# Retention followed by a squared-ReLU FFN: the second FFN product of seven blocks done as seven quarter products

## The chip, the cores and the metric

One core of one Trainium2 chip. A time is the device time of one execution in microseconds; lower is better. Engines: TensorE (PE; its weight loads are shown as PEld), VectorE (DVE), ScalarE (ACT), GpSimd (POOL) and SyncE (SP), which issues all of this kernel's DMAs. Each engine works through its own queue in the order in which the program was written.

## The reference

Four batches, eight heads, 768 steps, head size 64. A recurrent state is decayed and updated at each step, the result is laid out as 3072 tokens of 512 numbers, and a feed-forward network follows:

```python
for t in range(S):
    state = gamma[None, :, None, None] * state + np.einsum('bhd,bhe->bhde', k[:, :, t], v[:, :, t])
    y[:, :, t] = scale * np.einsum('bhd,bhde->bhe', q[:, :, t], state)
...
x = np.ascontiguousarray(attn_out.transpose(0, 2, 1, 3)).reshape(B * S, H * D)
h = np.maximum(x @ w_in, 0.0)          # w_in 512 x 2048
return (h * h @ w_out).astype(np.float32)   # w_out 2048 x 512
```

q, k, v, the weights and the result are fp32.

## The kernel before, in words

**Tiling.** The tokens are cut into 24 chunks of 128, six to a batch. `BLOCKS` groups them for the FFN: one block of four chunks (tb = 0) and ten of two (tb = 1 to 10). A chunk's attention is done in the chunked form: scores times mask, times v, plus q times the state so far. The matmuls take bf16 operands and sum in fp32 in PSUM.

**The order.** It is written out by hand. `ffn_pieces(tb)` (L786) is a generator; each `yield` ends a *place*, and `before(n)` (L984) then emits whatever `put` has entered for place n, and after it the squares of `take_squares` (L734). Places are numbered through: a two-chunk block has 16, block 1 those from 33 on, block 3 from 65, block 4 from 81, block 9 from 161. In such a block the first eight pieces are the first product: eight matmuls of 128 x 256 columns into one PSUM buffer (`first_product`, L754), then a ReLU on ScalarE (`relu`, L765) and a square on VectorE. The other eight are the second product: two chunks x 16 matmuls of 512 columns (`second`, L812), with a copy out of PSUM on ScalarE and a store behind each chunk (`store`, L823). The last eight places of a block thus take four 512-column matmuls each.

**Buffers.** PSUM has one buffer each for `tp`, `st`, `y` and `c_ps` and four in turn for `psf`, which both products use. `stage` is four fp32 buffers in turn, for the weights and for k and v of the later chunks.

**Attention from chunk 8 on** (`attend2`, L928), by d, the place of the chunk's outputs (70, 78, 86 and so on for chunks 10, 11, 12): q is scaled at d - 19 and d - 18 (even chunks), k at d - 18 (`scale_k2`, L618, VectorE, two instructions of 64 partitions, into a block-diagonal `ks_bdp`), v is cast at d - 15 (`cast_v2`, L631, POOL: once in full and twice by halves into a block-diagonal `v_bd`), k is transposed by DMA at d - 13, the state is updated at d - 6 and d - 3 (`state2`, L678; its PSUM is copied out by halves, one on ScalarE, one on VectorE), the scores are taken at d - 5 and the outputs at d.

**Loads.** k and v of three or four chunks come in eight DMAs (`batch_loads`, L120), one at each of the places in the table `places` (L971): chunks 15 to 17 of v at places 82 to 89, chunks 21 to 23 of v at 128 to 137. All wait in SP's queue among the transposes, the q loads and the stores.

**The weights of the second product** arrive in four quarters (`load_w_out`, L154; w_out rows in 16 blocks of 128) and are cast to bf16 at places 13, 17, 21 and 26 (`cast_w_out`, L300). Chunks 4 to 7 are attended in an earlier form (`attend`, L916; `scale_kv` L345, `transpose_k` L374, `scores` L396), and their items stand at places 21 to 49.

Of the kernel before, what the change touches and what calls it, by code (L numbers as in the profile page):

```python
# [22 lines left out]


PACK_FROM = 8


@with_exitstack
def kernel(
# [30 lines left out]
    const = ctx.enter_context(tc.tile_pool(name="const", bufs=1))  # L60
# [10 lines left out]

    stage = ctx.enter_context(tc.tile_pool(name="stage", bufs=4))
    opool = ctx.enter_context(tc.tile_pool(name="opool", bufs=4))
    ps_tp = ctx.enter_context(tc.tile_pool(name="ps_tp", bufs=1, space=bass.MemoryType.PSUM))
# [65 lines left out]
    halves = [slice(0, 64), slice(64, 128)]  # L140
    w_in_v = moe_w_in.rearrange("(cb p) f -> p cb f", p=P)
    w_out_v = moe_w_out.rearrange("(fb p) n -> p fb n", p=P)
    staged = {}
# [8 lines left out]
        staged["in", g] = t  # L152

    def load_w_out(g):  # L154
        t = stage_tile(FPQ * DM).rearrange("s (f n) -> s f n", f=FPQ)
        nc.sync.dma_start(t[:], w_out_v[:, g * FPQ : (g + 1) * FPQ, :])
        staged["out", g] = t

    load_q(0)
    load_pair(0, "kn", k, raw_k)  # L160
# [14 lines left out]
    def exponents(pattern, step, name, logs, parts=(slice(0, P),)):  # L175
# [27 lines left out]
        out=ident[:],  # L203
# [11 lines left out]
        out=cmask[:],  # L215
# [10 lines left out]
    for rows in halves:  # L226
        nc.gpsimd.affine_select(
            out=maskp[rows],
# [8 lines left out]
    kf2 = const.tile([P, NCH, 2, NPAIR], FP32)  # L237
# [44 lines left out]

    w_in_bf = [const.tile([P, NCB, FQ], BF16, name=f"w_in_bf{g}") for g in range(NQ)]
    w_out_bf = [const.tile([P, FPQ, DM], BF16, name=f"w_out_bf{g}") for g in range(NQ)]

    def cast_w(kind, g, halves=(0, 1), on="VVSG"):

# [327 lines left out]
            nc.vector.tensor_copy(to, fr)  # L615


    def scale_k2(m):  # L618
        b, i = chunks[m]
        ks = ks_bd2s[m % 2]  # L620
        kn = raw_k.pop(m)
        for hh, rows in enumerate(halves):
            nc.vector.tensor_tensor(  # L623
                out=ks[rows, :, hh, :].rearrange("s (u p) d -> s u p d", u=2),
                in0=kn[rows],
                in1=kf2[rows, i, :, :, None].to_broadcast([64, 2, NPAIR, D]),
                op=ALU.mult,
            )
        at[m]["ks"] = ks

    def cast_v2(m):  # L631
        vn = raw_v.pop(m)
        v2 = v2pool.tile([P, 2 * NPAIR, D], BF16, name="v2")
        nc.gpsimd.tensor_copy(v2.rearrange("s (u p) d -> s u p d", u=2), vn)  # L634
        v_bd = v_bd2s[m % 2]
        for hh, rows in enumerate(halves):
            nc.gpsimd.tensor_copy(  # L637
                v_bd[rows, :, hh, :].rearrange("s (u p) d -> s u p d", u=2), vn[rows]
            )
        at[m].update(v2=v2, v_bd=v_bd)  # L640

    def transpose_k2(m):
# [35 lines left out]
    def state2(m, u):  # L678

        b, i = chunks[m]  # L680
        a = at[m]
        if i == NCH - 1 and u == 1:
            return
        if i == 0 and u == 0:
            c_ps[0] = ps_c.tile([P, NPAIR, D], FP32, name="c_ps")
        c = c_ps[0]
        for p in range(NPAIR):
            nc.tensor.matmul(  # L688
                c[:, p, :],
                lhsT=a["ks"][:, u * NPAIR + p],  # L690
                rhs=a["v2"][:, u * NPAIR + p, :],
                start=(i == 0 and u == 0 and p == 0),
                stop=True,
                skip_group_check=True,
            )
        s_bd = s_bds[(2 * m + u) % 3]
        nc.scalar.activation(s_bd[halves[0], :, 0, :], c[halves[0]], AF.Copy)  # L697
        nc.vector.tensor_copy(s_bd[halves[1], :, 1, :], c[halves[1]])  # L698

    def outputs2(m):  # L700
        b, i = chunks[m]
# [30 lines left out]
    squares = []  # L732

    def take_squares():  # L734
        while squares:
            hv = squares.pop(0)
            nc.vector.tensor_mul(hv, hv, hv)  # L737


    h2s = {}  # L740
# [8 lines left out]
    def h_of(tb, f0, f1=None):  # L749
        n = NFB // len(h2s[tb])  # L750
        j, f = divmod(f0, n)
        return h2s[tb][j][:, f : f + (1 if f1 is None else f1 - f0)]
# [9 lines left out]
                stop=(cb == NCB - 1),  # L762
            )

    def relu(hv, hp):  # L765
        nc.scalar.activation(hv, hp[:], AF.Relu)  # L766
        squares.append(hv)

    open_ps = {}

# [15 lines left out]
    def ffn_pieces(tb):  # L786
        nch = BLOCKS[tb]
        TB = nch * C
        if tb == 0:
            for f in range(FPQ, NFB):  # L790
                hp = ps_f.tile([P, TB], FP32, name="psf")
                first_product(tb, hp[:], f, slice(0, TB))
                relu(h_of(tb, f)[:, 0], hp)
                yield
        elif tb <= 2:

            for c in range(nch):
                for g in range(NQ):
                    first_unit(tb, g, c)
                    yield  # L800
        else:
            h_tiles(tb)
            per = 512 // TB
            for f0 in range(0, NFB, per):
                hp = ps_f.tile([P, per, TB], FP32, name="psf")
                for f in range(f0, f0 + per):
                    first_product(tb, hp[:, f - f0, :], f, slice(0, TB))
                relu(h_of(tb, f0, f0 + per), hp)
                yield


        def second(op, j, g, cols=slice(0, DM)):  # L812
            for fq in range(FPQ):
                f = g * FPQ + fq
                nc.tensor.matmul(  # L815
                    op[:],
                    lhsT=h_of(tb, f)[:, 0, j * C : (j + 1) * C],
                    rhs=w_out_bf[g][:, fq, cols],
                    start=(f == 0),
                    stop=(f == NFB - 1),  # L820
                )

        def store(op, j, cols=slice(0, DM)):  # L823
            osb = opool.tile([P, DM], FP32, name="osb")
            nc.scalar.activation(osb[:, cols], op[:], AF.Copy)  # L825
            r0 = (first[tb] + j) * C
            nc.sync.dma_start(out[r0 : r0 + C, cols], osb[:, cols])
# [82 lines left out]
    def put(place, what, *args):  # L910
        parts.setdefault(place, []).append((what, args))
# [16 lines left out]
    def attend2(m, d, before, q_at, qturn_at, k_at, turn_at, v_at):  # L928
        if m % 2 == 0:
            put(q_at, scale_q, m, 0)  # L930
            put(q_at + 1, scale_q, m, 1)
            put(qturn_at, dma_transpose_q, m)
        put(k_at, scale_k2, m)
        put(v_at, cast_v2, m)
# [91 lines left out]
```

## Time and profile before

| | us |
|---|---|
| three runs | 213.21, 213.47, 214.4 (median 213.47) |
| the profiled execution: span from the first to the last instruction | 213.3 |
| TensorE busy / weight loads busy | 205.2 / 141.4 |
| VectorE / ScalarE / POOL busy | 134.7 / 117.0 / 57.9 |
| mean granted TensorE clock | 0.998 |

A span is read with its stages in mind: the first 20 us load and start, from 30 us on the FFN runs with attention between its pieces, and the last block has no attention beside it. In a line of the timeline the first number is the start, the second the time taken by the whole group, the bracket the idle time of that engine before it and what ended it. A matmul's time is longer than its distance to the next, since matmuls are pipelined; SPq is the time that SP spends on issuing.

### The profile page before, as it was taken

The numbers are of one execution on the slowest core, as the hardware profiler recorded it, in microseconds if no ns is written. First come the engines' busy times: TensorE is split into PE (matmuls) and PEld (weight loads), VectorE is DVE, ScalarE is ACT, GpSimd is POOL, SyncE is SP. The second block draws the span as 40 slices with busy tenths as digits, with TensorE's granted clock in tenths as the row PEclk, the third lists the DMA queues.
The fourth block names the chain that finished last, engine by engine and source line by source line (L and its number), as shares of the span: only waits on it lengthen the run. The fifth ranks groups of instructions, "written<-read, shape, count | busy, mean of one in ns | idle before, by whom it ended". The sixth has DMA issues, their size and how long they took to land.

```text
span 213.3 us, 5243 instructions
## 1 busy us (share of the span) xinstructions
PE 205.2 (96%) x2117; PEld 141.4 (66%) x2117; DVE 134.7 (63%) x263; ACT 117.0 (55%) x220; POOL 57.9 (27%) x114
## 2 busy tenths in 40 slices
PE   5798999999999999999999999999999999999994
PEld 1467744457965984884875875874965965965853
DVE  4677787235798997396495596595694793640410
ACT  8345887158953763662663663652753754643631
POOL 5232458223102523142230343052130433000000
PEclk9999999999999999999999999999999999999999
DMA  5999999999999997969978998959988451701102
GB/s 163 292 318 383 383 384 252 285 242 293 247 160 175 259 167 140 254 111 231 189 124 152 271 166 205 242 105 190 239 150 211 103 98 49 101 0 52 49 0 98
DMA packets 92727, 40.18 MB, mean 188 GB/s; under 512 B 68512, under 2 KB 86176, under 8 KB 92704
## 3 DMA queue, kind: packets, MB, share of 16 engines
q1 hardware_dynamic: 92704, 39.86, 83.1%
q8 instruction: 16, 0.26, 0.5%
q14 instruction: 7, 0.06, 0.1%
HBM read 27.26 MB, written 6.29 MB: 157 GB/s over the span
## 4 chain that ended last, share of the span: by engine, by line
PE 78%; DVE 8%; SPq 5%; DMA 4%; ACT 3%; issue 1%; ACTq 0%; DVEq 0%
PE psf L815 34%; PE psf L757 33%; SPq L132 4%; DMA kn<-in_k_dram 3%; DVE ks_bdp L623 2%; DVE h L737 2%; DMA stage<-in_v_dram 2%; PE y L717 2%; PE y L710 2%; PE st L661 2%; PE c_ps L688 1%; PE y L316 1%; PE c_ps L565 1%; DVE pt L548 1%; PE psf L524 1%
## 5 line engine op out<-in xcount | busy, mean ns | idle before, releaser
L757 PE MATMUL psf<-xt,w_in_bf 128*128 128x256 bf16 (+2 forms) x880 | 90.6, 259 | 0.2 <-ACT xt L488 0.2
L815 PE MATMUL psf<-w_out_bf,h 128*128 128x512 bf16 (+2 forms) x400 | 89.6, 371 | 0.0
L757 PEld LDWEIGHTS <-w_in_bf 128*128 128x128 bf16 x880 | 71.1, 98 | 11.6 <-issue 0.3
L766 ACT ACTIVATE h<-psf 128x512 bf16<-128x512 f32 x96 | 57.1, 597 | 22.2 <-PE psf L757 19.4
L815 PEld LDWEIGHTS <-h 128*128 128x128 bf16 x400 | 36.0, 98 | 35.7 <-DVE h L737 1.0
L737 DVE TENSOR_TENSOR h<-h 128x512 bf16<-128x512 bf16 x96 | 45.1, 492 | 17.8 <-ACT h L766 17.2
L698 DVE CAST s_bd<-c_ps 64x256 bf16<-64x256 f32 x29 | 12.4, 427 | 31.1 <-ACT s_bd L697 30.8
L637 POOL CAST v_bd<-stage 64x512 bf16<-64x512 f32 x32 | 23.2, 726 | 28.1 <-PE y L717 27.1
L825 ACT ACTIVATE osb<-psf 128x512 f32<-128x512 f32 (+2 forms) x25 | 14.5, 580 | 28.8 <-PE psf L815 28.8
L634 POOL CAST v<-stage 128x512 bf16<-128x512 f32 x16 | 11.3, 705 | 61.7 <-DMA stage<-in_v_dram 28.8
L623 DVE TENSOR_TENSOR ks_bdp<-stage,kf 64x512 bf16<-64x512 f32 x32 | 24.9, 779 | 0.6
L724 ACT ACTIVATE xt<-y 128x512 bf16<-128x512 f32 x16 | 11.9, 741 | 13.5 <-PE y L717 13.5
L335 DVE TENSOR_TENSOR qs<-qn,qf 128x512 bf16<-128x512 f32 x22 | 15.4, 709 | 2.3 <-DMA qn<-in_q_dram 2.0
L697 ACT ACTIVATE s_bd<-c_ps 64x256 bf16<-64x256 f32 x29 | 10.6, 367 | 10.3 <-PE c_ps L688 8.1
L411 DVE TENSOR_TENSOR pt<-st,cmask 128x512 bf16<-128x512 f32 x8 | 5.5, 689 | 10.1 <-PE st L404 10.1
L668 DVE TENSOR_TENSOR pt<-st,cmask 128x512 bf16<-128x512 f32 x16 | 11.1, 691 | 0.5
L304 POOL CAST w_out_bf<-stage 128x512 bf16<-128x512 f32 x12 | 8.3, 724 | 5.3 <-DMA stage<-in_moe_w_out_dram 5.3
L688 PEld LDWEIGHTS <-ks_bdp 128*128 128x128 bf16 x116 | 7.2, 98 | 3.4 <-issue 0.4
L717 PE MATMUL y<-pt,v_bd 128*128 128x64 bf16 x128 | 9.4, 193 | 0.0
L710 PE MATMUL y<-qT,s_bd 128*128 128x64 bf16 x120 | 9.1, 193 | 0.0
L710 PEld LDWEIGHTS <-s_bd 128*128 128x128 bf16 x120 | 8.2, 98 | 1.1
L717 PEld LDWEIGHTS <-v_bd 128*128 128x128 bf16 x128 | 8.1, 98 | 1.2
(99 smaller groups left out, 141.9 us busy)
## 6 DMA issues: line engine op xcount, KB each, us to landing
qn<-in_q_dram SPq DMA_DIRECT2D x12, 512.0 KB, 5.0
out_dram<-osb SPq DMA_DIRECT2D x23, 256.0 KB, 3.8
stage<-in_moe_w_out_dram SPq DMA_DIRECT2D x4, 1024.0 KB, 8.0
stage<-in_moe_w_in_dram SPq DMA_DIRECT2D x3, 1024.0 KB, 11.7
stage<-in_k_dram SPq DMA_DIRECT2D x32, 96.0 KB, 3.6
stage<-in_v_dram SPq DMA_DIRECT2D x32, 96.0 KB, 3.3
kn<-in_k_dram SPq DMA_DIRECT2D x2, 512.0 KB, 6.8
vn<-in_v_dram SPq DMA_DIRECT2D x2, 512.0 KB, 7.5
```

The lines of the kernel that those rows point to most:

```text
L335: engine.tensor_tensor(out=out, in0=by, in1=table[:, :, None].to_broadcast([P, H, D]), op=ALU.mult)
L623: nc.vector.tensor_tensor(out=ks[rows, :, hh, :].rearrange("s (u p) d -> s u p d", u=2), in0=kn[rows], in1=kf2[rows, i, :, :, None].to_bro ...
L637: nc.gpsimd.tensor_copy(v_bd[rows, :, hh, :].rearrange("s (u p) d -> s u p d", u=2), vn[rows])
L698: nc.vector.tensor_copy(s_bd[halves[1], :, 1, :], c[halves[1]])
L710: nc.tensor.matmul(yv, lhsT=s_bds[(2 * m + u - 1) % 3][:, p], rhs=half_of(a["qT"], p, u), start=True, stop=False,)
L717: nc.tensor.matmul(yv, lhsT=a["v_bd"][:, u * NPAIR + p], rhs=a["pt"][:, u * NPAIR + p, :].rearrange("s (r t) -> s r t", r=2), start=not inter,
L724: nc.scalar.activation(xts[tb][:, :, off : off + C].rearrange("e p (s r) -> e p r s", r=2), y[:], AF.Copy,)
L737: nc.vector.tensor_mul(hv, hv, hv)
L757: nc.tensor.matmul(hp, lhsT=w_in_bf[g][:, cb, fq * 128 : (fq + 1) * 128], rhs=xts[tb][:, cb, cols], start=(cb == 0), stop=(cb == NCB - 1),)
L766: nc.scalar.activation(hv, hp[:], AF.Relu)
L815: nc.tensor.matmul(op[:], lhsT=h_of(tb, f)[:, 0, j * C : (j + 1) * C], rhs=w_out_bf[g][:, fq, cols], start=(f == 0), stop=(f == NFB - 1),)
L825: nc.scalar.activation(osb[:, cols], op[:], AF.Copy)
```

## The change

Blocks 3 to 9 (`SEVEN`) compute the second product by Strassen's method in Winograd's form. The block's h is seen as 2 x 2 quarters (chunk by even or odd f block), w_out as 2 x 2 quarters (even or odd f block by column half); seven products of quarters, each eight matmuls of 256 columns, take the place of the eight that 2 x 2 by 2 x 2 has (32 matmuls of 512 columns). That needs:

- four sums of quarters of w_out (`sum_w_out`), formed once: for each of the four weight quarters four VectorE operations and two ScalarE copies, at places 24 and 25 (all four at once for the first two), 37 to 40 and 43 to 46. They work in the unused end of the weights' `stage` buffer;
- four sums of quarters of h per block, on VectorE: `s1`, `s2` in two parts, `s3`, `s4` whole, into block-diagonal tiles that are no longer in use (s3 in place);
- sums of the products: in PSUM where an accumulation can go on, else on VectorE (`u`, `v`, two halves of `ob`, one of `oa`), with two quarter copies on ScalarE. The seventh product and its store are kept until the next block's second piece;
- in these blocks two of the eight squares (pieces 2 and 4) move to ScalarE.

For all chunks from 8 on, `scale_k2` becomes `cast_k2` (POOL, two plain casts into the block-diagonal tile), and `cast_v2` becomes `scale_v2`: VectorE scales v in full, and POOL copies its halves into `v_bd`. Both halves of the state's copy out of PSUM are on ScalarE.

```diff
+SEVEN = range(3, 10)
...
+    def sum_w_out(g):
+
+        src, (t3, t2) = staged["out", g], (staged["rest", g][:, w] for w in range(2))
+        b11, b12 = src[:, ::2, 0:HN], src[:, ::2, HN:DM]
+        b21, b22 = src[:, 1::2, 0:HN], src[:, 1::2, HN:DM]
+        to = [t[:, 2 * g : 2 * g + 2] for t in sums]
+        add = nc.vector.tensor_tensor
+        yield add(out=t3, in0=b22, in1=b12, op=ALU.subtract)
+        yield add(out=t2, in0=t3, in1=b11, op=ALU.add)
+        nc.scalar.activation(to[2], t3, AF.Copy)
+        yield add(out=to[0], in0=b12, in1=b11, op=ALU.subtract)
+        nc.scalar.activation(to[1], t2, AF.Copy)
+        yield add(out=to[3], in0=b21, in1=t2, op=ALU.subtract)
...
-    def scale_k2(m):
-        b, i = chunks[m]
+    def cast_k2(m):
...
-            nc.vector.tensor_tensor(
-                out=ks[rows, :, hh, :].rearrange("s (u p) d -> s u p d", u=2),
-                in0=kn[rows],
-                in1=kf2[rows, i, :, :, None].to_broadcast([64, 2, NPAIR, D]),
-                op=ALU.mult,
+            nc.gpsimd.tensor_copy(
+                ks[rows, :, hh, :].rearrange("s (u p) d -> s u p d", u=2), kn[rows]
             )
...
-    def cast_v2(m):
+    def scale_v2(m):
+        b, i = chunks[m]
...
-        nc.gpsimd.tensor_copy(v2.rearrange("s (u p) d -> s u p d", u=2), vn)
+        nc.vector.tensor_tensor(
+            out=v2.rearrange("s (u p) d -> s u p d", u=2),
+            in0=vn,
+            in1=kf2[:, i, :, :, None].to_broadcast([P, 2, NPAIR, D]),
+            op=ALU.mult,
+        )
...
-            nc.gpsimd.tensor_copy(
-                v_bd[rows, :, hh, :].rearrange("s (u p) d -> s u p d", u=2), vn[rows]
-            )
+            nc.gpsimd.tensor_copy(v_bd[rows, :, hh, :], v2[rows])
...
-        nc.vector.tensor_copy(s_bd[halves[1], :, 1, :], c[halves[1]])
+        nc.scalar.activation(s_bd[halves[1], :, 1, :], c[halves[1]], AF.Copy)
...
+            hv, on_scalar = squares.pop(0)
+            if on_scalar:
+                nc.scalar.activation(hv, hv, AF.Square)
+            else:
+                nc.vector.tensor_mul(hv, hv, hv)
...
+        def first_sums(js):
+            add(s1[:, js], a21[:, js], a22[:, js])
+            add(s2[:, js], s1[:, js], a11[:, js], ALU.subtract)
+
+        def rest():
+            first_sums(slice(4, 8))
+            pa = ps_tp.tile([P, HN], FP32, name="tp")
+            pb, pe, pd = (ps_f.tile([P, HN], FP32, name="psf") for _ in range(3))
...
+            for js, stop in ((range(0, 6), False), (range(6, 8), True)):
+                product(pa[:], a11, b11, js, True, stop)
+                product(pe[:], a22, t4, js, True, stop)
+                if stop:
+                    nc.scalar.activation(a[:], pa[:], AF.Copy)
+                yield
+            add(s3, a11, a21, ALU.subtract)
+            product(pd[:], s1, t1, range(8), True, True)
+            yield
+            add(s4, a12, s2, ALU.subtract)
+            product(pb[:], s2, t2, range(8), True, True)
+            add(u[:], pb[:], a[:])
+            yield
+            for js in (range(0, 4), range(4, 8)):
+                product(pa[:], a12, b21, js, False, js[-1] == 7)
+                if js[0]:
+                    nc.scalar.activation(oa[:, 0:HN], pa[:], AF.Copy)
+                yield
+            for js in (range(0, 4), range(4, 8)):
+                product(pb[:], s3, t3, js, False, js[-1] == 7)
+                if js[0]:
+                    add(v[:], pb[:], a[:])
+                    add(ob[:, HN:DM], pd[:], v[:])
+                    add(ob[:, 0:HN], pe[:], v[:])
+                    nc.sync.dma_start(out[r0 + C : r0 + 2 * C], ob[:])
+
+                    def last_product():
+                        product(pd[:], s4, b22, range(8), False, True)
+                        add(oa[:, HN:DM], pd[:], u[:])
+                        nc.sync.dma_start(out[r0 : r0 + C], oa[:])
+
+                    kept.append(last_product)
+                yield
...
-                relu(h_of(tb, f0, f0 + per), hp)
+                relu(h_of(tb, f0, f0 + per), hp, tb in SEVEN and f0 // per in (1, 3))
+                if f0 == per and kept:
+                    kept.pop()()
+                if f0 // per == 5 and tb in SEVEN:
+                    first_sums(slice(0, 4))
                 yield
+            if tb in SEVEN:
+                yield from rest()
+                return
...
+    for g, at_places in enumerate(((24, 24, 24, 24), (25, 25, 25, 25), (37, 38, 39, 40), (43, 44, 45, 46))):
+        made = sum_w_out(g)
+        for place in at_places:
+            put(place, next, made)
```

More of the change, by code (lines that the diff above doesn't have):

```diff
@@ L73 @@
     opool = ctx.enter_context(tc.tile_pool(name="opool", bufs=4))
+    upool = ctx.enter_context(tc.tile_pool(name="upool", bufs=1))
     ps_tp = ctx.enter_context(tc.tile_pool(name="ps_tp", bufs=1, space=bass.MemoryType.PSUM))
@@ L154, in load_w_out @@
     def load_w_out(g):
-        t = stage_tile(FPQ * DM).rearrange("s (f n) -> s f n", f=FPQ)
+        whole = stage.tile([P, 2 * NCH * NPAIR * D], FP32, name="stage")
+        t = whole[:, 0 : FPQ * DM].rearrange("s (f n) -> s f n", f=FPQ)
         nc.sync.dma_start(t[:], w_out_v[:, g * FPQ : (g + 1) * FPQ, :])
         staged["out", g] = t
+        staged["rest", g] = whole[:, FPQ * DM :].rearrange("s (w j n) -> s w j n", w=2, n=DM // 2)
     load_q(0)
@@ L284 @@
     w_out_bf = [const.tile([P, FPQ, DM], BF16, name=f"w_out_bf{g}") for g in range(NQ)]
+    HN = DM // 2
+    sums = [const.tile([P, NFB // 2, HN], BF16, name=f"w_sum{i}") for i in range(4)]
+    def sum_w_out(g):
[10 more added lines that the diff above has]
+        yield add(out=to[3], in0=b21, in1=t2, op=ALU.subtract)
     def cast_w(kind, g, halves=(0, 1), on="VVSG"):
@@ L735, in take_squares @@
         while squares:
-            hv = squares.pop(0)
-            nc.vector.tensor_mul(hv, hv, hv)
+            hv, on_scalar = squares.pop(0)
[3 more added lines that the diff above has]
+                nc.vector.tensor_mul(hv, hv, hv)
     h2s = {}
@@ L763, in first_product, with relu, seven_products, add @@
             )
-    def relu(hv, hp):
+    def relu(hv, hp, on_scalar=False):
         nc.scalar.activation(hv, hp[:], AF.Relu)
-        squares.append(hv)
+        squares.append((hv, on_scalar))
+    kept = []
+    def seven_products(tb):
+        h = h2s[tb][0].rearrange("e (j k) (c t) -> e k c j t", k=2, c=2)
+        a11, a12, a21, a22 = h[:, 0, 0], h[:, 1, 0], h[:, 0, 1], h[:, 1, 1]
+        s1, s2, s4 = (
+            t.rearrange("s p hh d -> s (p hh d)").rearrange("s (j t) -> s j t", t=C)
+            for t in (k_bds[0], k_bds[1], v_bds[0])
+        )
+        s3 = a21
+        t1, t2, t3, t4 = sums
+        b11, b21, b22 = (
+            lambda j, k=k, n=n: w_out_bf[j // 2][:, 2 * (j % 2) + k, n * HN : (n + 1) * HN]
+            for k, n in ((0, 0), (1, 0), (1, 1))
+        )
+        def add(out, in0, in1, op=ALU.add):
+            nc.vector.tensor_tensor(out=out, in0=in0, in1=in1, op=op)
+        def product(to, left, right, js, start, stop):
+            for j in js:
+                nc.tensor.matmul(
+                    to,
+                    lhsT=left[:, j],
+                    rhs=right(j) if callable(right) else right[:, j],
+                    start=(start and j == 0),
+                    stop=(stop and j == NFB // 2 - 1),
+                    skip_group_check=True,
+                )
+        def first_sums(js):
[5 more added lines that the diff above has]
+            pb, pe, pd = (ps_f.tile([P, HN], FP32, name="psf") for _ in range(3))
+            oa, ob = (opool.tile([P, DM], FP32, name="osb") for _ in range(2))
+            a, u, v = (upool.tile([P, HN], FP32, name=f"u{i}") for i in range(3))
+            r0 = first[tb] * C
+            for js, stop in ((range(0, 6), False), (range(6, 8), True)):
[29 more added lines that the diff above has]
+                yield
+        return first_sums, rest
@@ L803, in ffn_pieces @@
             per = 512 // TB
+            if tb in SEVEN:
+                first_sums, rest = seven_products(tb)
             for f0 in range(0, NFB, per):
@@ L807, in ffn_pieces @@
                     first_product(tb, hp[:, f - f0, :], f, slice(0, TB))
-                relu(h_of(tb, f0, f0 + per), hp)
+                relu(h_of(tb, f0, f0 + per), hp, tb in SEVEN and f0 // per in (1, 3))
[3 more added lines that the diff above has]
+                    first_sums(slice(0, 4))
                 yield
+            if tb in SEVEN:
+                yield from rest()
+                return
         def second(op, j, g, cols=slice(0, DM)):
@@ L932, in attend2 @@
             put(qturn_at, dma_transpose_q, m)
-        put(k_at, scale_k2, m)
-        put(v_at, cast_v2, m)
+        put(k_at, cast_k2, m)
+        put(v_at, scale_v2, m)
         put(turn_at, transpose_k2, m)
```

## The prediction, as it was put down before the changed kernel ran

> **What bounds the kernel now.** I read the page first (busy times, chain, groups), then the groups kept apart by shape, then TensorE's timeline for the gap from one matmul to the next, then the other engines' timelines at the places the diff touches.
>
> ```profile
> span 213.3 us, 5243 instructions
> PE 205.2 (96%) x2117; PEld 141.4 (66%) x2117; DVE 134.7 (63%) x263; ACT 117.0 (55%) x220; POOL 57.9 (27%) x114
> PE psf L815 34%; PE psf L757 33%; SPq L132 4%; DMA kn<-in_k_dram 3%; DVE ks_bdp L623 2%; DVE h L737 2%; DMA stage<-in_v_dram 2%; PE y L717 2%; PE y L710 2%; PE st L661 2%; PE c_ps L688 1%; PE y L316 1%; PE c_ps L565 1%; DVE pt L548 1%; PE psf L524 1%
> ```
>
> Two thirds of the chain are the two FFN products. A busy matmul unit need not be a saturated one, so the gaps decide:
>
> ```profile
> 112.97 2.75 PE L815 MATMUL psf<-w_out_bf,h 128*128 128x512 bf16 x12
> 105.20 2.79 PE L757 MATMUL psf<-xt,w_in_bf 128*128 128x256 bf16 x24
> ```
>
> Twelve 512-column matmuls start within 2.75 - 0.38 us (0.38 being one's duration), 216 ns apart; twenty-four 256-column ones within 2.79 - 0.27, 109 ns apart. Each has its own weight load of 98 ns, which therefore hides under 109 ns too. From 30 to 205 us TensorE is busy 174.5 of 175 us: it streams, and nothing else is late for more than 0.2 us. So matmul columns removed count in full, and so does every wait put in TensorE's way.
>
> **What the products save.** Of a block, 32 matmuls x 216 ns = 6.91 us become 7 x 8 = 56 x 109 ns = 6.10 us. Seven blocks: 7 x 0.81 = **-5.66 us**. This is certain as far as the rate holds (bounds -5.5 to -5.8).
>
> **The weight sums, first half (places 24, 25).** Eight VectorE operations on 512 fp32; nearest row L335 (128x512 fp32 in), 0.68 us, 0.62 to 0.65 apart in a run: 8 x 0.65 = 5.2 us. They depend on loads alone and follow `ks` at 38.6 us, where VectorE now idles 6.56 us until L411 at 45.19: hidden. Their four ScalarE copies are not: they stand ahead of chunk 4's `k_bd` copies.
>
> ```profile
> 43.24 1.21 ACT L385 ACTIVATE k_bd<-tp 64x512 bf16<-64x512 bf16 x2 [0.93 <-PE tp L378]
> ```
>
> The `qT` copy ahead ends at 42.3; four copies 0.52 apart (L306, 1.14 for two) end at 44.4, `k_bd` at 45.5 in place of 44.45. TensorE's L404 takes it at 44.77: **+0.8 us** (0 to 1.2).
>
> **The weight sums, second half (places 37 to 40, 43 to 46).** From 57.88 to 63.18 VectorE runs without a gap, and TensorE already waits for its last item, chunk 7's `ks`:
>
> ```profile
> 62.51 0.67 DVE L335 TENSOR_TENSOR ks<-kn,kf 128x512 bf16<-128x512 f32 x1
> 63.24 0.40 PE L378 MATMUL tp<-ident,ks 128*128 128x128 bf16 x4 [0.18 <-DVE ks L335]
> ```
>
> Four sums of 0.62 us come ahead of it: **+2.5 us** (1.5 to 2.9). The other four fall where k's scaling (1.4 us a chunk, L623) leaves VectorE: nothing (up to 0.5).
>
> **A block's own work.** By rows, VectorE before: 8 squares at 0.42 (L737), 4 half-scalings at 0.69 (L623), 2 q scalings, 2 masks, 4 state copies at 0.43: 10.6 us per 15.7 us. After: 6 squares, 2 scalings of v at 0.7, q and masks as they were, six operand sums (four of 512 elements at 0.42; two of 1024: twice the streamed part, some 0.7; bounds 0.42 to 0.84), five adds out of PSUM at 0.43 (64x256 copy, L698): 11.9 us per 14.9. ScalarE gains two squares, four state copies (0.37) and two quarter copies, and loses two stores: 9.0 to 11.2 us. Both fit. Laying the items in order from the end of the eighth piece, the last square is done at +1.25 us and wanted at +1.67, `s3` at 3.6 and wanted at 5.3, `u` at 4.8 and wanted at 5.3. These margins of 0.4 to 1.7 us are the cover; POOL can eat into it. A square takes 424 ns alone (68 of 96) and 721 in the middle while a POOL cast runs (28 of 96), 830 at most; k's casts now fall beside `s3` and `s4`. I take 0.15 us a block not already standing in a longer wait, in five blocks: **+0.8 us** (0 to 3). The Trainium skill (SBUF — State Buffer, "Who interferes with whom") says why: a VectorE instruction with two SBUF inputs contends with a GpSimd instruction that reads SBUF, for the whole instruction; the trace agrees with 424 against 721 ns, and by the rule all six operand sums are exposed, which with 0.3 us each on the path would be an estimated 12 us more, far above what I take, since most lie in the margins.
>
> **v's scaling changes engines, and this is what I expect to decide.** POOL's v cast sits waiting for its load, and nobody minds, as v is wanted nine places later. `scale_v2` stands on VectorE, whose next items at that place are `v`, `ob`, `ob`.
>
> ```profile
> 102.93 0.34 SPq L827 DMA_DIRECT2D out_dram<-osb  x1
> 106.02 3.61 SPq L132 DMA_DIRECT2D stage<-in_v_dram  x4
> 115.08 0.64 SPq L132 DMA_DIRECT2D stage<-in_v_dram  x1
> 117.75 0.28 PE L688 MATMUL c_ps<-v,ks_bdp 128*128 128x64 bf16 x4
> 120.41 0.61 POOL L634 CAST v<-stage 128x512 bf16<-128x512 f32 x1 [10.06 <-DMA stage<-in_v_dram]
> ...
> 150.00 0.34 SPq L827 DMA_DIRECT2D out_dram<-osb  x1
> 160.56 0.64 SPq L132 DMA_DIRECT2D stage<-in_v_dram  x1
> 164.82 0.28 PE L688 MATMUL c_ps<-v,ks_bdp 128*128 128x64 bf16 x4
> 165.63 0.61 POOL L634 CAST v<-stage 128x512 bf16<-128x512 f32 x1 [8.21 <-DMA out_dram<-osb]
> ```
>
> Chunk 15's v is scaled at place 95, one place (0.86 us) before the L688 at 117.75: 116.9. It lands at 120.0 (the wait before the cast at 120.41 ends then): 3.1 us late. Why: after the store at 102.93, which waits for the block's end at 102.05, SP has 12.1 us of issues without a gap (loads, transposes, a q load) and the last v needs 5 us to land. After the change, counted from that block's end on TensorE: the store is ready at 1.5, not 0.9 (`scale_v2` done, `v`, `ob`, `ob` after the last matmul at 0.2 + 3 x 0.43), one store more (0.6) stands in between, so v lands at 1.5 + 12.1 + 0.6 + 5.0 = 19.2. TensorE reaches place 95 after 8.76 (first products and attention, as now) + 0.87 (the kept product) + 4.8 (44 matmuls x 109) = 14.4. VectorE then needs 1.27 us (0.7 scaling, 0.43 `v`, starts) before `pb` is free, which the next block's second piece takes: 1.67 us after place 95 if nothing waits. The wait: 4.8 + 1.27 - 1.67 = 4.4, less 0.4 for small waits that it swallows: **+4.0 us** (0 to 5). For chunk 21 (place 143) the same count with 10.6 us of issues gives 17.4 against 14.4: 2.6, less 0.4: **+2.2 us** (0 to 3.5). The other chunks' v lands in time (chunk 18 at 138.4 for 140.3), the first four far ahead.
>
> **The clock.** It was 1.00 up to 212.44 us and 0.50 from there, 2 us after the last matmul; that stretch of 3.4 us (209.02 to 212.44) had 1.30 us of matmul. A wait of 4 us leaves a stretch like it somewhere, so TensorE should lose half of a 3.4 us stretch behind it: **+1.7 us** (0 to 5, if the other waits do it too). The Trainium skill (TensorE: Matmul & The Clock Gate, "What's actually happening") has it as a free-running window of 3.4 us and half rate after an idle one; the trace agrees: the full clock begins at 14.465, and 58 windows later is 212.44. Taken literally, only a wholly idle window counts, and a 4 us wait holds one about one time in six: then this term would be 0 in most cases, and the sum 218.1.
>
> **Sum** against the profiled execution, whose span is 213.3 us; the runs' median is 213.47, so 0.2 us lies around it: 213.3 - 5.66 + 0.8 + 2.5 + 0.8 + 4.0 + 2.2 + 1.7 = 219.6, and **219.8 us** as a run's time.
>
> **Rivals.**
> (a) *The loads land in time.* If SP runs ahead, since it no longer stops for a store in mid-block (1.05 us before the one at 99.02), and v lands within 0.4 us of its place (the point from which it decides, 1.67 - 1.27), both waits and the clock term go: 213.3 - 5.66 + 0.8 + 2.5 + 0.8 + 0.2 = **211.9**, faster. For it: the sums' delay gives SP 3.3 us. Against: the store at the block's end ties SP to TensorE again.
> (b) *The sums hide as well*, because VectorE or ScalarE takes them earlier than the order above: **208.6**. Against it: both queues are strictly in order in the trace.
> (c) *Only chunk 15 waits, and not long* (under 2 us, no clock loss): 211.9 + 1 to 2 = **213.5**, no change.
> (d) *VectorE's operand sums wait for POOL's casts, and the clock bites more often*: 0.5 us in each of seven blocks and two more halved stretches: 219.8 + 2.7 + 3.4 less overlap = **224**.
>
> **Chances.** Forecast 0.56 (own range 215.5 to 222.5), (a) 0.19, (b) 0.08, (c) 0.09, (d) 0.08. The range takes in (a), (c) and most of the forecast's upper bounds: 210 to 223. A measurement of this kernel can tell some 0.5%, 1.07 us. Faster: (a) and (b), 0.27; same 0.08; slower 0.65.
>
> **What would show it.** Matmuls of the second product 109 ns apart; an L404-like wait of TensorE for `k_bd` near 45 us; `ks` ending near 66 us and the transposes waiting for it; VectorE idle on `stage<-in_v_dram` near places 95 and 143 with TensorE idle at the next block's second piece; a clock of 0.5 in the slice after. If TensorE stays 98% busy past 70 us, the load theory is wrong and the result is (a) or (b). If the 256-column matmuls come slower than 109 ns, the whole sum rises by 0.39 us per ns.

## The result, and the profile after

The changed kernel takes **224.94 us** (median of 224.02 to 226.68, four runs) against 213.34 for the kernel before (213.21 to 214.4, four runs): a ratio of 1.054 (95%: 1.049 to 1.059). It is slower, as forecast, but by 11.6 us and not by 6.3, and it lies outside the range, which ended at 223.0. Times here are medians of all runs; the ratios leave out single runs well above the others (the longest took 428.1 and 522.49 us).

The page of the changed kernel; the third line is the matmul unit's busy share in tenths over forty slices of 5.6 us, the fourth the granted clock in the same slices, the fifth and sixth the chain of waits by engine and by line:

```profile
span 223.0 us, 5683 instructions
PE 203.1 (91%) x2285; PEld 158.8 (71%) x2285; DVE 148.9 (67%) x297; ACT 136.9 (61%) x271; POOL 70.9 (32%) x130
PE   4889999799959999999999299999999499999994
PEclk9999999999988999999999979999999999999999
PE 69%; DMA 9%; DVE 9%; issue 6%; ACT 3%; SPq 1%; POOL 1%; DVEq 0%
PE psf L783 30%; PE psf L817 12%; PE psf L928 11%; PE tp L817 5%; DMA qn<-in_q_dram 5%; DMA kn<-in_k_dram 3%; DMA stage<-in_v_dram 2%; PE y L740 1%; PE st L684 1%; PE y L733 1%; PE c_ps L711 1%; POOL ks_bdp L645 1%; DVE stage L303 1%; ACT k_bd L408 1%; DVE stage L302 1%
```

Read the slices first. TensorE was full from 30 us on; now four slices are not: a 7 at about 41 us, a 5 at 64, a 2 at 124 and a 4 at 175, with the clock's 8 8 and 7 behind the second and the third. Between 30 us and the last slice everything else is full. The lines of VectorE around the deepest hole (the first and third are the adds `u` and `v`, the fourth both halves of `ob`):

```profile
118.43 0.41 DVE L813 TENSOR_TENSOR u<-psf,u 128x256 f32<-128x256 f32 x1
...
125.24 0.69 DVE L654 TENSOR_TENSOR v<-stage,kf 128x512 bf16<-128x512 f32 x1 [6.40 <-DMA qn<-in_q_dram]
125.85 0.42 DVE L813 TENSOR_TENSOR u<-psf,u 128x256 f32<-128x256 f32 x1
126.30 0.76 DVE L813 TENSOR_TENSOR osb<-psf,u 128x256 f32<-128x256 f32 x2
```

and TensorE in the same stretch:

```profile
121.60 1.03 PE L783 MATMUL psf<-xt,w_in_bf 128*128 128x256 bf16 x8
126.78 1.58 PE L817 MATMUL psf<-w_out_bf,v_bd 128*128 128x256 bf16 x8 [4.15 <-DVE osb L813]
```

This is the forecast mechanism. `scale_v2` (L654) of chunk 15 stands 6.40 us at the head of VectorE's queue; the bracket names a q load, but what it needs is the last v load, which SP issued at 119.82, right behind that q load, and which lands at 124.97. Behind it stand the adds `v`, `ob`, `ob`, and `last_product`, which adds into the bank that the second of these reads, waits 4.15 us. The clock in the stretch of 3.41 us that holds most of the wait, and in the one behind it (stretch, its length, busy PE with its matmuls, clock, share of the DMA engines, GB/s):

```profile
123.69:127.11 3.42, 0.33 (x4) 1.00 0.40 54
127.11:130.52 3.41, 3.41 (x22) 0.50 0.67 167
```

TensorE does 22 matmuls behind the wait, where the next 3.41 us hold 45: 1.7 us more.

The second hole, at 64 us, is made by the weight sums: one of them stands just ahead of chunk 7's `ks`, for which TensorE waits, and the clock halves behind it too (stretches as above).

```profile
64.97 0.67 DVE L307 TENSOR_TENSOR w_sum<-stage 128x512 bf16<-128x512 f32 x1
65.56 0.68 DVE L358 TENSOR_TENSOR ks<-kn,kf 128x512 bf16<-128x512 f32 x1
```

```profile
66.30 0.61 PE L401 MATMUL tp<-ident,ks 128*128 128x128 bf16 x4 [1.92 <-DVE ks L358]
```

```profile
62.26:65.67 3.41, 1.50 (x13) 1.00 0.76 142
65.67:69.08 3.41, 2.78 (x10) 0.50 1.08 211
```

The fourth hole, at 175 us, is chunk 21's `last_product`, which waits like chunk 15's:

```profile
176.84 1.03 PE L817 MATMUL psf<-w_out_bf,v_bd 128*128 128x256 bf16 x8 [2.74 <-DVE osb L813]
```

**Where the time went.** I took the distance from each matmul's start to the next, less its usual distance; what is over is time lost (so a wait here is some 0.15 us longer than in its bracket).

| place | lost, us |
|---|---|
| two waits for `k_bd`, 42.9 to 45.0 | 1.8 |
| waits for a mask product `pt` and for `ks` of chunk 7, 63.2 to 66.3 | 2.9 |
| clock halved behind them, 65.67 to 69.08 | 1.35 |
| chunk 15: `kT` 0.6, `last_product` 4.3 | 4.9 |
| clock halved behind them, 127.11 to 130.52 | 1.7 |
| chunk 21: a relu of ScalarE 0.6, `last_product` 2.9 | 3.5 |
| small waits in the blocks, over those of the kernel before | 0.8 |
| seven products for eight, worked out before | -5.66 |
| sum | 11.3 |

The medians differ by 11.6.

### The profile page after: what moved, and what is told of

It is laid out like the page before. It is cut to its first block, busy times and chain, and to the rows that moved or that the text cites. A ratio compares the mean times of both kernels' runs of the same rounds, so it can differ in the third digit from the quotient of the medians.

```text
span 223.0 us, 5683 instructions
## 1 busy us (share of the span) xinstructions
PE 203.1 (91%) x2285; PEld 158.8 (71%) x2285; DVE 148.9 (67%) x297; ACT 136.9 (61%) x271; POOL 70.9 (32%) x130
## 4 chain that ended last, share of the span: by engine, by line
PE 69%; DMA 9%; DVE 9%; issue 6%; ACT 3%; SPq 1%; POOL 1%; DVEq 0%
PE psf L783 30%; PE psf L817 12%; PE psf L928 11%; PE tp L817 5%; DMA qn<-in_q_dram 5%; DMA kn<-in_k_dram 3%; DMA stage<-in_v_dram 2%; PE y L740 1%; PE st L684 1%; PE y L733 1%; PE c_ps L711 1%; POOL ks_bdp L645 1%; DVE stage L303 1%; ACT k_bd L408 1%; DVE stage L302 1%
## 5 line engine op out<-in xcount | busy, mean ns | idle before, releaser
L662 POOL COPY v_bd<-v 64x512 bf16<-64x512 bf16 x32 | 21.1, 659 | 59.7 <-DVE v L654 51.7
L928 PE MATMUL psf<-w_out_bf,h 128*128 128x512 bf16 (+2 forms) x176 | 38.3, 368 | 0.0
L645 POOL CAST ks_bdp<-stage 64x512 bf16<-64x512 f32 x32 | 24.5, 767 | 29.0 <-issue 23.3
L928 PEld LDWEIGHTS <-h 128*128 128x128 bf16 x176 | 16.3, 100 | 15.6 <-issue 1.6
L654 DVE TENSOR_TENSOR v<-stage,kf 128x512 bf16<-128x512 f32 x16 | 11.1, 695 | 12.0 <-DMA qn<-in_q_dram 6.4
L817 PE MATMUL tp<-w_out_bf,h 128*128 128x256 bf16 x112 | 15.8, 273 | 0.0
L817 PE MATMUL psf<-w_sum,h 128*128 128x256 bf16 x112 | 15.6, 272 | 0.1
L720 ACT ACTIVATE s_bd<-c_ps 64x256 bf16<-64x256 f32 x29 | 10.7, 369 | 6.3 <-PE c_ps L711 6.3
L817 PE MATMUL psf<-w_sum,k_bd 128*128 128x256 bf16 x112 | 13.8, 273 | 0.0
L938 ACT ACTIVATE osb<-psf 128x512 f32<-128x512 f32 (+2 forms) x11 | 6.1, 558 | 11.3 <-PE psf L928 11.2
L817 PEld LDWEIGHTS <-k_bd 128*128 128x128 bf16 x112 | 10.6, 98 | 1.3
L721 ACT ACTIVATE s_bd<-c_ps 64x256 bf16<-64x256 f32 x29 | 11.0, 379 | 0.4
```

The lines of the kernel that those rows point to most:

```text
L645: nc.gpsimd.tensor_copy(ks[rows, :, hh, :].rearrange("s (u p) d -> s u p d", u=2), kn[rows])
L654: nc.vector.tensor_tensor(out=v2.rearrange("s (u p) d -> s u p d", u=2), in0=vn, in1=kf2[:, i, :, :, None].to_broadcast([P, 2, NPAIR, D]), ...
L662: nc.gpsimd.tensor_copy(v_bd[rows, :, hh, :], v2[rows])
L721: nc.scalar.activation(s_bd[halves[1], :, 1, :], c[halves[1]], AF.Copy)
L817: nc.tensor.matmul(to, lhsT=left[:, j], rhs=right(j) if callable(right) else right[:, j], start=(start and j == 0), stop=(stop and j == NF ...
L928: nc.tensor.matmul(op[:], lhsT=h_of(tb, f)[:, 0, j * C : (j + 1) * C], rhs=w_out_bf[g][:, fq, cols], start=(f == 0), stop=(f == NFB - 1),)
```

## The experiments

Times are medians; the ratio is to the kernel before on the same chip, with its 95% interval. "After" is the changed kernel. All compute the full output; run h also has matmuls whose result is not used.

| run | us | ratio |
|---|---|---|
| after | 224.94 | 1.054 (1.049 to 1.059) |
| a_v_later: v scaled six places later | 213.1 | 0.998 (0.994 to 1.001) |
| b_sums_moved: weight sums behind the attention's items | 221.49 | 1.032 (1.025 to 1.040) |
| c_both: a and b together | 208.88 | 0.978 (0.976 to 0.979) |
| d_no_seven: the change without the seven products | 213.74 | 1.001 (0.999 to 1.003) |
| e_v_first: after, v loaded ahead of k | 216.04 | 1.011 (1.007 to 1.015) |
| f_kv_as_before: b, k and v on their old engines | 213.66 | 1.000 (0.997 to 1.002) |
| g_engines_as_before: f, half the state copies on VectorE | 225.17 | 1.055 (1.051 to 1.059) |
| h_stands: c and six deliberate waits | 235.72 (one run) | |
| i_state_as_before: c, half the state copies on VectorE | 215.66 | 1.009 (1.006 to 1.012) |
| j_eight_blocks: c, block 2 by seven products too | 211.67 | 0.992 (0.989 to 0.995) |
| k_eight_tuned: j, two sums later | 212.25 | 0.992 (0.989 to 0.995) |

### Is it the place of v's scaling, and of the sums? (a, b, c)

The theory: an instruction that waits for a load stands ahead of adds that TensorE needs; so putting it six places later must take the waits at chunks 15 and 21 away, with nothing else of the change touched.

```diff
-                *ahead.get(m, (d - 19, d - 16, d - 18, d - 13, d - 15)))
+                *ahead.get(m, (d - 19, d - 16, d - 18, d - 13, d - 9)))
```

> The changed kernel with one number altered: v of chunks 12 on is scaled six places later (d - 9 in place of d - 15). Theory (VectorE's queue stands at v's load, twice): the changed kernel lost 4.9 us of TensorE time at chunk 15, 3.5 at chunk 21 and 1.7 to the halved clock behind the first; all of it goes: 224.9 - 10.1 = 214.8, and no gap of TensorE over 0.6 us after 70 us. Rival (VectorE is simply overfull and short of its port, so that the waits only move): less than half of it goes, 220 or more.

213.1 us, 11.8 less than the changed kernel for one number of the source. Past 70 us TensorE loses no more than 0.81 us in one place. The wait for `ks` is as it was; in the profiled execution the clock does not halve behind it, which accounts for most of the gap to the 214.8 expected. Whether it halves probably spreads the runs: seven of 212.24 to 213.33 us had a mean clock of 1.00, two of 214.7 and 214.82 had 0.99, as one halved stretch would make it (3.41 x 0.5 / 213 = 0.008). That was not seen in a trace of those two.

Run b leaves v alone and takes the sums out of the way: they are put behind the attention's items of the same place, and those of the second half lie two to five places later.

```diff
-    for g, at_places in enumerate(((24, 24, 24, 24), (25, 25, 25, 25), (37, 38, 39, 40), (43, 44, 45, 46))):
...
+    for g, at_places in enumerate(((24, 24, 24, 24), (25, 25, 25, 25), (41, 42, 44, 45), (46, 47, 48, 48))):
```

> The changed kernel with the weight sums placed otherwise: the first half behind the attention items of places 24 and 25, the second half at places 41, 42, 44 to 48, behind chunk 7's scaling of k. Theory (the sums stand ahead of what TensorE waits for): 1.8 us at k_bd, 2.9 at ks and 1.4 of halved clock go, 0.3 may come at the scores of place 46: 224.9 - 5.8 = 219.1. Rival (the sums cost the same wherever they are, as VectorE has no room): 223 or more.

221.49 us. The waits for `ks` and `k_bd` fall to 0.33 and 0.22 us, but 0.71 us comes up at the scores of place 29, and the waits for v are still there (3.59 and 2.22 us, the clock halved behind each). It is 2.4 us over the 219.1 expected, mostly for a wait of TensorE that the changed kernel does not have. Chunk 12's v, scaled at 94.98 us, stands 1.88 us for its load, which lands at 94.71 (the bracket names another); two squares are queued behind it, and TensorE takes both:

```profile
94.98 0.69 DVE L654 TENSOR_TENSOR v<-stage,kf 128x512 bf16<-128x512 f32 x1 [1.88 <-PE st L684]
95.59 1.16 DVE L763 TENSOR_TENSOR h<-h 128x512 bf16<-128x512 bf16 x2
```

```profile
96.07 0.28 PE L817 MATMUL tp<-w_out_bf,h 128*128 128x256 bf16 x1 [1.27 <-DVE h L763]
96.81 0.28 PE L817 MATMUL tp<-w_out_bf,h 128*128 128x256 bf16 x1 [0.46 <-DVE h L763]
```

By distance between starts these two cost 2.1 us. So a stand hurts in front of squares as well as in front of adds. Both edits together:

> Both edits together. Theory: 224.9 - 10.1 - 5.8 = 209.0, which is before's 213.3 less the 5.7 us that the products save, plus 1 to 1.5 us of small waits. Rival (256-column products do not save what their rate says, or the small waits of seven blocks eat it): 212 or more.

**208.88 us**, 4.5 below the kernel before, the fastest version of the study. VectorE at the end of the same block in run c, where chunk 14's v is now scaled, and then chunk 15's:

```profile
111.89 0.42 DVE L813 TENSOR_TENSOR u<-psf,u 128x256 f32<-128x256 f32 x1 [0.26 <-PE psf L817]
112.23 1.08 DVE L654 TENSOR_TENSOR v<-stage,kf 128x512 bf16<-128x512 f32 x1
114.03 0.42 DVE L813 TENSOR_TENSOR u<-psf,u 128x256 f32<-128x256 f32 x1 [0.71 <-PE psf L817]
...
120.55 0.68 DVE L654 TENSOR_TENSOR v<-stage,kf 128x512 bf16<-128x512 f32 x1
```

A v scaling still stands ahead of an add, but neither has a bracket: the loads have landed (chunk 15's at 118.52), and the add waits for TensorE, as it should. Over 80 us of the main part (busy PE, PEld, DVE, ACT and POOL with their counts, clock, share of the DMA engines) the kernel before and run c read

```profile
100.00:180.00 80.00, 80.00 (x811) 56.80 (x810) 54.39 (x99) 42.89 (x80) 22.39 (x32) 1.00 0.86 170
```

```profile
100.00:180.00 80.00, 79.53 (x964) 71.85 (x962) 64.27 (x122) 56.19 (x116) 27.43 (x41) 1.00 0.87 175
```

TensorE is full again, with VectorE at 80% in place of 68%.

### Does the late load cost anything by itself? (d, e)

Run d keeps everything of the change but the products: `SEVEN` is empty, and there are no weight sums. v is scaled on VectorE at the changed kernel's place.

```diff
-SEVEN = range(3, 10)
+SEVEN = range(0)
```

> The changed kernel without its products and weight sums: all blocks take the old second product, but k is cast on POOL, v scaled on VectorE at its old place and the state copied by ScalarE. Theory (a late v costs only because the adds that free TensorE's next operands stand behind it): VectorE still waits about 3 us for chunk 15's v, TensorE does not, 213.3 within 0.8. Rival (moving the scaling is bad by itself): 216 or more, with gaps of TensorE of 3 us near places 95 and 143.

213.74 us, no change. And here the same stand is to be seen:

```profile
117.81 0.69 DVE L654 TENSOR_TENSOR v<-stage,kf 128x512 bf16<-128x512 f32 x1 [7.65 <-DMA out_dram<-osb]
118.42 0.69 DVE L691 TENSOR_TENSOR pt<-st,cmask 128x512 bf16<-128x512 f32 x1
```

VectorE stands 7.65 us for chunk 15's v, longer than in the changed kernel, and TensorE loses nothing over 0.3 us in any place past 70 us: without the seven products ScalarE empties the banks, and what is queued behind the stand (a mask, two squares) is wanted later. So the cost is not the stand; it is the stand ahead of what TensorE wants next: here adds that free PSUM, in run b squares. c less d, 4.9 us, is what the products themselves save, of 5.66 worked out; the rest fits the small waits.

Run e attacks the load in place of the instruction: the changed kernel with the second half of v loaded before the second half of k.

```diff
-        (12, "k"): [47, 48, 49, 50, 52, 53, 55, 56] + [74 + j for j in range(8)],
-        (12, "v"): [58, 59, 60, 61, 62, 64, 65, 66] + [82 + j for j in range(8)],
+        (12, "k"): [47, 48, 49, 50, 52, 53, 55, 56] + [82 + j for j in range(8)],
+        (12, "v"): [58, 59, 60, 61, 62, 64, 65, 66] + [74 + j for j in range(8)],
...
-        (18, "k"): [92 + 4 * j // 3 for j in range(8)] + [117 + 4 * j // 3 for j in range(8)],
-        (18, "v"): [103 + 4 * j // 3 for j in range(8)] + [128 + 4 * j // 3 for j in range(8)],
+        (18, "k"): [92 + 4 * j // 3 for j in range(8)] + [128 + 4 * j // 3 for j in range(8)],
+        (18, "v"): [103 + 4 * j // 3 for j in range(8)] + [117 + 4 * j // 3 for j in range(8)],
```

> The changed kernel with only the loads' order altered: chunks 15 to 17 and 21 to 23 load v at the eight places where k's loads stood, and k at v's. v is scaled at its old place. Theory (it is the lateness of v, whoever waits): v lands in time, so the 4.9, 3.5 and 1.7 us go; now POOL waits for k, and nothing that TensorE wants soon stands behind that: 224.9 - 10.1 = 214.8, up to 217 if k's transposes by DMA come late for the scores. Rival (it was moving the scaling six places that helped, by unloading VectorE at that place): 222 or more.

216.04 us: the waits at chunks 15 and 21 are gone (nothing over 0.64 us past 70 us), those for `k_bd` and `ks` stay. In its profiled execution, 219.09 us and the longest of the seven, the clock halves behind both of these. Two independent edits, one of the order and one of the loads, take the same 9 to 12 us away; that settles the cause.

### Were the moves between engines needed? (f, g, i)

Run f is c with k's scaling back on VectorE and v's cast back on POOL. The cast is also back at its old place, d - 15, since a late v was taken not to matter there. I expected little cost.

```diff
-        put(k_at, cast_k2, m)
-        put(v_at, scale_v2, m)
+        put(k_at, scale_k2, m)
+        put(v_at, cast_v2, m)
```

> Both edits of the two runs together (v late is no matter here: it is cast by POOL at d - 15), but k is scaled on VectorE and v cast on POOL as before the change; the state copies stay on ScalarE. By rows VectorE then has 11.9 - 1.4 + 2.8 = 13.3 us of work in a block of 14.9. Theory (only a wait in front of TensorE costs): POOL takes v's wait, 209 to 211. Rival (the scaling had to move for VectorE to have room): 213 or more.

213.66 us: my theory fell, the rival holds. Runs g and i put the state's second half copy back on VectorE, in g on top of f, in i alone on top of c:

```diff
-        nc.scalar.activation(s_bd[halves[1], :, 1, :], c[halves[1]], AF.Copy)
+        nc.vector.tensor_copy(s_bd[halves[1], :, 1, :], c[halves[1]])
```

> The same with one half of the state copies back on VectorE: 15.0 us of VectorE work by rows in a block of 14.9. Theory: VectorE becomes the bound and TensorE waits for its adds in every block, 0.5 to 1 us each: 212 to 216. Rival (the engine moves were not needed at all): 209 to 210.

> Both edits (the 208.9 us kernel), with one half of the state copies back on VectorE and nothing else. By rows VectorE then has 11.9 + 1.7 = 13.6 us of work in a block of 14.9, as little more as the run that put only k's and v's scaling back (13.3) and cost 4.8. Theory A (an overfull VectorE is what costs, and margins shrink with its work): 213 to 215. Theory B (a state copy stands in VectorE's queue for TensorE and ScalarE, so that the work is not the measure): 217 or more. Theory C (only both moves undone overfill it): 209 to 211.

225.17 and 215.66 us. Run g is far above the 212 to 216 expected of it, and run i falls between its theories A and B, so it decides for neither. Over the same 80 us, f, g and i in this order:

```profile
100.00:180.00 80.00, 77.01 (x927) 68.58 (x926) 69.16 (x129) 53.68 (x111) 25.12 (x32) 1.00 0.88 167
```

```profile
100.00:180.00 80.00, 74.46 (x874) 64.88 (x875) 71.02 (x138) 43.38 (x84) 21.63 (x27) 1.00 0.86 169
```

```profile
100.00:180.00 80.00, 76.99 (x911) 67.41 (x910) 66.82 (x134) 46.72 (x90) 29.21 (x41) 1.00 0.87 167
```

In f, VectorE waits for a load only once there, 0.8 us for a q. With VectorE 84 to 89% busy TensorE loses 3 to 5.5 of the 80 us, and the lists of waits in that stretch (the one that waits and the one waited for, us in total, times, longest) say for what, g's TensorE first, then i's VectorE:

```profile
PE tp L817 <- DVE h L763: 6.3, 6, 1.6
```

```profile
DVE s_bd L721 <- ACT s_bd L720: 6.7, 5, 1.3
```

The last squares of a block come late. In i the list puts VectorE's longest idle time on its copy of half a state, behind ScalarE's half, up to 1.3 us; what is queued behind that copy stands with it, squares too. The kernel before had the same wait in the same 80 us, 13 times and 21.4 us in all, with TensorE busy throughout: again a stand that cost nothing until the products needed VectorE. That this wait, and not VectorE's greater load alone, makes the squares late was not tried by itself. Taken back alone, k and v cost 4.8 us and the state copies 6.8, together 16.3, which is more than the sum. So each of these moves is needed for the products to pay in full, and what was wrong with v's was its place.

### What does a wait cost beyond itself? (h)

Run c with a row of clears on VectorE and one small matmul that waits for them, at six places; the matmul's result goes nowhere.

```diff
+    def stand(times):
+        for _ in range(times):
+            nc.vector.memset(slack[:], 0.0)
+        st = ps_st.tile([P, 2 * NPAIR, C // 2], FP32, name="st")
+        nc.tensor.matmul(st[:, 0, :], lhsT=ident[:], rhs=slack[:, 0:64], start=True, stop=True)
+
+    for place, times in ((90, 2), (106, 6), (122, 12), (138, 8), (154, 10), (170, 14)):
+        put(place, stand, times)
```

> Both edits together, plus six waits put in on purpose, one a block (places 90 to 170): VectorE clears a small buffer 2, 6, 12, 8, 10 and 14 times, and one extra matmul into the scores' buffer waits for it (its result is not used). TensorE stands some 0.5 to 3 us each time. Theory from the runs so far (the clock halves for 3.4 us behind a stretch of the 3.413 us grid in which TensorE was busy less than some 43%): one to three halved stretches. Rival (only a wholly idle stretch counts): none, as no wait reaches 3.4 us.

The waits came out longer than the 0.5 to 3 us that were meant: 1.20, 2.37, 4.69, 2.95, 3.53 and 4.71 us, 19.5 in sum. The span is 26.8 us over that of c, and behind the waits five stretches of 3.41 us had half the clock: (26.8 - 19.5) / 5 = 1.5 us for each (1.6 if a wait of 0.6 us at 115 us, which c has and h has not, is counted). The rival, that only a wholly idle stretch counts, falls. The wait of 2.37 us halved one, in a stretch with 35% of matmul; the longer one of 2.95 us did not, as it fell across two stretches (46% and 72%).

### Can more be had? (j, k)

Run j gives block 2 the seven products as well; run k also moves two of its sums to places 29 and 30.

```diff
-SEVEN = range(3, 10)
+SEVEN = range(2, 10)
```

> Both edits, and block 2 takes the seven products too (its h sums stand behind the seventh first-product unit and at its rest). Theory (a product's columns count in full while VectorE has its margin; in block 2's second half it has little else to do): 208.9 - 0.8 = 208.1, up to 208.6 with small waits. Rival (VectorE is too full there, as chunk 7 and 8 are near): 209 or more.

> As the run with eight blocks, with two of the weight sums of place 25 moved to 29 and 30, out of the way of the mask that the scores of place 29 wait for (0.71 us of TensorE's time there with both edits): 0.3 to 0.7 less than that run, 207.4 to 207.8. Rival (that wait lies beside the start's spread or moves to place 33): no difference.

211.67 and 212.25 us: slower than c by some 3, against a saving expected of under one. There is no trace of j at this speed, so the places are read in k. There TensorE waits 1.29 us, up to 50.81, for ScalarE's `xt`, which stands behind the copies of the two moved sums; and in block 2

```profile
78.51 0.39 PE L817 MATMUL psf<-w_sum,h 128*128 128x256 bf16 x2 [0.28 <-DVE h L763]
79.26 0.39 PE L817 MATMUL psf<-w_sum,h 128*128 128x256 bf16 x2 [0.35 <-DVE h L763]
81.50 0.39 PE L817 MATMUL psf<-w_sum,h 128*128 128x256 bf16 x2 [1.86 <-DVE h L763]
```

its products stand for squares, which in that block are all on VectorE. No order in which the eighth block pays was tried.

## Why the prediction was right in kind and short in size

The step that failed is the sizing of the waits, and most of all the count of halved stretches; the mechanism held. The clock term stood for one halving (1.7 us) and there were two (3.05); the waits at chunks 15 and 21 stood at 6.2 and cost 8.4 (7.2 without two small waits beside them); the first half of the weight sums stood at 0.8 and cost 1.8. Term by term:

- **Products, -5.66:** right. The second product's 256-column matmuls start 110 ns apart (six in 0.82 us, less 0.27), and c less d gives 4.9 with the small waits in it.
- **Weight sums, first half, +0.8:** 1.8 measured, above its upper bound of 1.2. I counted ScalarE's copies back to back, 0.52 us apart; two of them wait for VectorE's sums, which take up to 1.10 us where I had 0.65:

```profile
38.59 1.10 DVE L302 TENSOR_TENSOR stage<-stage 128x512 f32<-128x512 f32 x1
```

```profile
42.25 0.63 ACT L304 ACTIVATE w_sum<-stage 128x512 bf16<-128x512 f32 x1 [0.52 <-DVE stage L302]
```

- **Second half, +2.5:** 2.9, at its upper bound; one of its sums takes 1.10 us too, at 62.24.
- **Small waits, +0.8:** 0.8. The Trainium skill's rule (SBUF — State Buffer, "Who interferes with whom") shows in the durations: the groups of the 512-element sums `s1` and of the 1024-element `s4` have means of 547 and 919 ns in the changed kernel, where 420 and 680 are undisturbed. That is 0.1 to 0.2 us for one operation on the mean. The prediction has the hold last for the whole instruction; the runs show 0.3 to 0.4 us beside casts and copies of 0.6 to 0.8 on POOL. And the estimate of 12 us by the rule did not come, as the prediction said: most of these operations lie in margins of 0.4 to 1.7 us. Runs f, g and i, with more work on VectorE, lose time in the blocks, which fits margins that can be used up.
- **Chunk 15, +4.0 and chunk 21, +2.2:** the mechanism holds, with 4.9 and 3.5 us. What the prediction put wrongly is the instruction that waits. It named the next block's second piece, through `pb`; that piece ran at 121.60, before `v` had read `pb`, so it takes another bank. The one held up is `last_product` behind it, which adds into the bank that `ob`'s add has to read first, 0.4 us later in VectorE's queue. By itself that makes the wait shorter, by some 0.5 us, as the piece (0.87 us) runs first. What made it longer is the load: counted from the block's end on TensorE (104.74 and 156.20 us) it landed at 20.2 and 18.8 us, where 19.2 and 17.4 were forecast. For chunk 15, a transposition took SP 2.19 us and the q load 1.41, where the kernel before had 1.30 and 0.59. The table's 4.9 and 3.5 also hold a wait for `kT` and one for a relu, 0.6 us each, which the forecast did not name. Rivals (a) and (c) are out, as the loads landed late for both chunks; (b) is out by the 1.8 and 2.9 us.
- **The clock, +1.7:** 1.7 behind chunk 15. The step failed in *how often*: I took one long wait to be needed, and the wait of 2.1 us for `ks` (with 0.8 just before it) halved a second stretch, 1.35 us more. The bounds of that term, 0 to 5, held it; rival (d) had more frequent halving, but gave it to sums that wait for POOL's casts; that its 224 is nearest to the measured time is luck.
- **The base:** two errors that offset each other, by luck. A run lies 1.8 us above its span (224.77 and 223.0 here, 208.87 and 207.0 in run c), not 0.2; and the profiled execution of before, whose clock came up at 14.46 us and not at 11.06 as in the changed kernel, had its first second product 1.6 us later (34.60 against 32.98). I had set the span of one execution against the runs of others.

The misses add up: 1.0 + 0.4 + 0.9 + 1.3 + 1.35 = 4.95 us, with 0.15 for the base, and 224.94 less 219.84 is 5.1. All have the same sign. The forecast's own range ended at 222.5, as if the misses of its terms would offset each other, though several of them hang together: the clock halves more often because the waits are longer, and chunk 15 has the `kT` wait besides.

## What to carry to other kernels

When work is moved to another engine, look first at what is queued *behind* it there: an instruction that waits for a load costs nothing on a queue whose next items are wanted late (7.65 us for nothing in run d), and its wait where they free PSUM for TensorE or make its operands (4.3 us lost for a stand of 6.40 at chunk 15, 2.1 for one of 1.88 in run b). The mend is its place in the order or the order of the loads, not taking the move back. And where several waits are added, look whether they lengthen together, and count the half clock with each.

## What the runs showed of the hardware that was not expected

- **The clock changes only on a fixed grid of 3.413 us**, in all traces read here, and a stretch need not be empty to halve the next one. Past the first 20 us every stretch with 0 to 40% of matmul halved it, and so did two with 44 and 45%; those with 43, 46, 55 to 64% and more did not. So a single threshold on this share does not sort them between 43 and 45%. The starts of runs f, h and k do not fit either (55, 60 and 61%, halved). Back to full it went after a halved stretch of 82% or more; after one of 76% (run h) it stayed. The Trainium skill (TensorE: Matmul & The Clock Gate, "What's actually happening") asks for an idle window; the traces disagree, by these shares, and agree with its window of 3.4 us.
- **A square or sum of two SBUF tiles takes 0.3 to 0.4 us more while POOL casts** (sums of 512 fp32: 0.69 and 1.10 us; squares in the kernel before: 0.42 and 0.72 us), less than the 0.61 us that the v cast of the kernel before took. The products with the mask, which read one input from PSUM, take 0.69 us alone and 0.68 beside POOL.
